# Paired DMA transposes, a tile's blocks side by side, outputs issued by ScalarE, 128 columns last, and a new order in a fused spectral filter and MLP kernel

## The chip, the cores and the metric

The kernel runs on one core of a Trainium2 chip. The metric is the time of one execution on the device in microseconds (us), the median of several runs. A profile of one execution shows the five engines: TensorE (PE, with its weight loads as PEld), VectorE (DVE), ScalarE (ACT), GpSimd (POOL) and SyncE (SP). SP and ScalarE also issue DMAs, shown as SPq and ACTq.

## The reference

`A_x` has 2048 rows of 512 values in bfloat16. Two results of it are mixed, row by row, with a gate:

```
x = A_x
g = sigmoid((x * gate_w).sum(-1, keepdims=True))
X = rfft2(x.astype(float32), axes=(-2, -1)) * (A_w_r + 1j * A_w_i)
a = irfft2(X, s=(2048, 512), axes=(-2, -1)).astype(bfloat16)
h = einsum("bsd,df->bsf", x, B_w1) + B_b1
act = h * tanh(softplus(h))
b = einsum("bsf,fd->bsd", act, B_w2)
out = g * a + (1 - g) * b
```

`B_w1` is 512 x 1792, `B_w2` 1792 x 512, and `A_w_r`, `A_w_i` are 2048 x 257.

## The kernel before

The rows are cut into 16 tiles of 128 (tile t holds the rows t, t+16, t+32 and so on, L447), and four tiles make a chunk c. All of the work is a list of named tasks, each with its engine, its reads and writes and the PSUM banks it needs. A string, `ORDER` (L300), gives one order of all tasks; the tokens of one engine, in their order, are that engine's program. A token is name:engine:bank. Before an instruction an engine waits on semaphores for the tasks that it depends on and for the last users of its bank (`place`, L221, and `emit`, L259). A token's place in the string sets nothing across engines beyond that.

The tasks by name, with number 0 to 15 for a tile where one stands:

- `x0`, `x2`, `x4`, `x8`, `x12` load x (L516), from 2 to 4 tiles each; `w1_*` and `w2_*` load the MLP's weights, `wr..s.` and `wi..s.` (L532) the filter's weights into a staging area, in six pieces of 257 KB, two of 249 and two of 8, `ldM` and `ldG` (L617, L619) constant matrices of 512 KB, `cFD` (L513) one of 128 KB.
- The MLP wants x transposed, in `xT`. Tiles 0 to 7 are transposed on TensorE (`tr`, L552 and L554, four matmuls of 128 columns) and copied out of PSUM (`evx`, L475, on ScalarE or VectorE). Tiles 8 to 15 are transposed by a DMA from HBM (`xt`, L534 and L462). `m{c}_{f}` (L800) is the first layer for chunk c and one of 14 pieces of 128 hidden units: four matmuls of 512 columns. The first four pieces of chunk 0 run as halves a and b. `h{c}_{f}` (L805, ScalarE) applies bias and activation. `n{t}` (L828) is the second layer for a tile, 14 matmuls of 512 columns; for tile 15 it is two tasks, `n15_0` with 384 columns and `n15_384` with 128.
- The spectral half runs in stages with DMAs between them: `bf` (L567, VectorE, sums and differences of x; bf4 and later do four tiles at once) and `p` (L577), `d` (L591), the shuffle DMAs `sh` (L613), `t` (L676), the filter on VectorE (`p1`, `p2`, `ad`), the edge step `e1` to `e3` (L709 to L739), `it` (L750), the DMAs `hx` (L758), `id` (L774) and `ip` (L812). The copies out of PSUM are `ep`, `ed`, `et`, `eit` and `ec`, all by L475.
- `gwb`, one matmul of 512 columns (L537), spreads the gate's weights, and `gt` (L599) makes the gate's sums.
- A tile of the output is written twice in SBUF: `o` scales the first of its two parts (L817, L818), and `s` adds the second (L822). Then `out` is issued, for two tiles at once (L846), for tile 14 alone (L848), and for tile 15 in two parts of 384 and 128 columns (L841).

Three things set the order around the change. TensorE, ScalarE and VectorE run their own lists strictly in order. SP's DMAs are issued in order too, and those with data dependencies (`sh`, `wrn`, `hx`, `out`) hold up what is behind them. PSUM has eight banks, and a token's bank is free when its last user is done.

Of the kernel before, what the change touches and what calls it, by code (L numbers as in the profile page):

```python
# [300 lines left out]
cRF:act ones:pool ident:pool ebase:pool x0:sp x2:sp w1_0a:sp warm:pe:0 fl0:pe:1
tr0:pe:0 gwl:act braw:act w1_0b:sp x4:sp bf0_0:dve bf0_1:dve tab:act w1_4:sp
x8:sp tr1:pe:1 evx1:act evx0:dve p0:pe:2 p1:pe tr2:pe:0 w1_9:sp x12:sp
wr0s1:sp wi0s2:sp wi0s0:sp wr0s2:sp cFD:sp wr0s0:sp ldM0:sp bf2_0:dve bf2_1:dve
tr3:pe:1 p2:pe:4 p3:pe tr_b:pe:6 evx3:dve ev_b:dve evx2:act fl1:pe:7 m0_2a:pe:1
m0_1a:pe:0 m0_1b:pe m0_2b:pe m0_3a:pe:6 m0_0a:pe:7 m0_3b:pe m0_0b:pe ep2:act ep0:dve
h0_2:act h0_1:act h0_3:act gwb:pe:0 bf4_0:dve bf4_1:dve tr4:pe:1 evx4:dve p4:pe:2
tr7:pe:6 p5:pe evx7:dve ep4:dve tr5:pe:4 m0_6:pe:1 tr6:pe:6 h0_0:act evx5:act
evx6:dve m0_8:pe:4 bf8_1:dve bf8_0:dve xt8:sp xt9:sp xt10:sp h0_8:act h0_6:act
gwe:act xt11:sp gt0:dve p6:pe:2 m1_8:pe:6 p7:pe p8:pe:4 p9:pe ep8:dve  # L310
ep6:act h1_8:act m0_7:pe:1 h0_7:act m1_7:pe:0 m1_5:pe:2 h1_5:act p10:pe:4 p11:pe
m1_0:pe:1 ep10:act h1_0:act bf12_1:dve bf12_0:dve gt1:dve p14:pe:2 p12:pe:6 p15:pe
p13:pe m1_4:pe:4 m0_4:pe:1 gt2:dve ep12:dve gt3:dve ep14:act d6:pe:2 d14:pe:6
gt4:dve h1_7:act h1_4:act h0_4:act ldM1:sp d7:pe gt5:dve d2:pe:4 d15:pe
# [7 lines left out]
gt14:dve h0_12:act h1_10:act t0_0:pe:2 gt15:dve wip0:pool wip1:pool wim000:dve zcl:dve
t0_1:pe wi1s0:sp wr1s0:sp et0:act m0_9:pe:1 ez:pool wrm010:dve wr1s1:sp wi1s1:sp
m1_11:pe:0 wrp0:pool wrp1:pool m2_8:pe:4 h1_11:act h2_8:act wim011:dve wim001:dve wim010:dve
t3_0:pe:2 t3_1:pe et3:act h2_4:act h2_6:act m1_6:pe:0 m2_7:pe:4 h2_0:act h2_7:act
h0_9:act h1_6:act xt12:sp xt13:sp ez1:dve win0:dve wic0:dve wiz0:dve xt14:sp
xt15:sp wrn00:sp wrn01:sp t2_0:pe:2 t2_1:pe p20_0:dve:0 et2:dve wim110:dve m2_1:pe:5
# [12 lines left out]
h3_6:act ad_6:dve p1_5:dve p27_0:dve:2 p27_1:dve ad_4:dve p1_7:dve ad_5:dve ad_7:dve  # L340
edge:sp e1:pe:2 o2_0:dve n0_0:pe:6 h3_2:act xp1:dve:0 xp20:dve:1 xp21:dve ead:dve:2
o0_0:act e2:pe:5 e3:dve m3_8:pe:4 ldG1:sp inv:sp ldG2:sp ldG0:sp it2_0:pe:0
it1_0:pe:2 ldG3:sp it1_1:pe it0_0:pe:6 it2_1:pe it0_1:pe eit1:dve eit0:dve h3_8:act
eit2:act n3_0:pe:4 it5_0:pe:0 it5_1:pe it3_0:pe:2 it3_1:pe eit3:dve eit5:act it4_0:pe:6
it4_1:pe n15_384:pe:5 eit4:act it6_0:pe:0 it6_1:pe it7_0:pe:2 it7_1:pe eit6:dve eit7:act
hx4_1:act hx4_0:act o3_0:act n4_0:pe:6 o4_0:dve hx12_0:act n5_0:pe:4 id6:pe:0 hx12_1:sp
rft:sp hx8_1:sp id7:pe o5_0:dve ec6:dve:0 id4:pe:2 id5:pe ec4:act:1 n7_0:pe:6
ey6_1:dve ey6_0:dve ey4_1:dve ey4_0:dve id12:pe:0 id13:pe id14:pe:2 id15:pe ip4:pe:4
n12_0:pe:7 s4:dve hx8_0:sp hx0_0:sp o7_0:act ec14:act:0 ey14_1:dve ec12:act:1 hx0_1:act
ey12_0:dve ey12_1:dve ip13:pe:4 id10:pe:0 id11:pe ip12:pe:6 ec10:act:1 o13:act o12:act  # L350
ey14_0:dve ey10_0:dve ey10_1:dve s12_0:dve ip15:pe:2 o15:dve n11_0:pe:3 id8:pe:0 id9:pe
ip11:pe:2 ip5:pe:4 id0:pe:6 id1:pe s15_384:dve n13_0:pe:5 ec8:act:0 s5:dve ey8_0:dve
ey8_1:dve ec0:act:1 out15_384:sp ey0_0:dve ey0_1:dve id2:pe:0 id3:pe ip10:pe:4 ip14:pe:6
o14:dve out5:sp n14_0:pe:7 o10:act o11:dve s11_0:dve s13_0:dve ip6:pe:6 n10_0:pe:5
ip1:pe:4 ec2:act:0 ey2_0:dve s14_0:dve ey2_1:dve ip3:pe:7 ip2:pe:0 ip9:pe:1 ip8:pe:3
n8_0:pe:2 s10_0:dve s1:dve s6:dve o9:act out11:act s3:dve s2:dve out3:act
ip7:pe:0 ip0:pe:1 o8:dve s0:dve s7:dve out1:act out7:act n9_0:pe:3 s9_0:dve
# [4 lines left out]
def _build(nc, A_x, A_w_r, A_w_i, B_x, B_w1, B_b1, B_w2, gate_w, out, XTP=8, LATE=8, NWARM=13, TRM=4,
# [10 lines left out]
    with es:  # L373
# [163 lines left out]
        G.add("gwb", "small", dict(pe=lambda e: e.matmul(bank(gb), one[0:1, :], junk[0:1, :], start=True, stop=True)), ("pe", 1, 512), reads=["gwl"], writes=[gb])  # L537
# [6 lines left out]
        for t in range(XTP):  # L544
            b = _Buf("b1")

            def f_tr(e, t=t, b=b):
                ins = None
                for dt_ in range(4):
                    xs = x_sb[:, t, 128 * dt_:128 * (dt_ + 1)]  # L550
                    if t < TRM:
                        ins = e.matmul(bank(b)[:, 128 * dt_:128 * (dt_ + 1)], xs, identt[:, :], start=True, stop=True)  # L552
                    else:
                        ins = e.transpose(bankb(b)[:, 128 * dt_:128 * (dt_ + 1)], xs, identt[:, :])  # L554
# [235 lines left out]
        for c in range(NCH):  # L790
            dph = {0: [], 1: [], 2: t_sh, 3: t_mv}[c]
            for ft in range(NFT):
# [3 lines left out]
                for h in ((0, 1) if split else (2,)):  # L796
                    def f_mm1(e, c=c, ft=ft, b=b, h=h):
                        ins = None
                        for dt_ in (range(4) if h == 2 else range(2 * h, 2 * h + 2)):
                            ins = e.matmul(bank(b), w1_sb[:, dt_, 128 * ft:128 * (ft + 1)], xT[:, c, dt_, :, :], start=(dt_ == 0), stop=(dt_ == 3))  # L800
# [98 lines left out]
```

## Time and profile before

| | us |
|---|---|
| median of 3 runs | 131.04 (130.96 to 131.35) |
| the profiled execution | 130.94 |
| its span (first to last event) | 129.17 |
| PE busy | 124.5, 96% of the span |
| DVE busy | 95.6, 74% |
| ACT busy | 71.8, 56% |
| share of TensorE's clock granted | 1.0 |

The span is what the profile's clock shows of that execution; 1.77 us of its time lie around it. "Busy" of PE is made of modelled ends: a matmul of 512 columns is shown with 0.38 us, while the next begins earlier. The chain that ended last is the path followed back from the last instruction.

### The profile page before, as it was taken

The page shows a single profiled execution, that of the slowest core. Times are in us where ns is not written, and L with a number is a line of the kernel's source. Part 1 is how long each engine was busy: PE and PEld are TensorE (multiplying, and loading weights), DVE is VectorE, ACT ScalarE, POOL GpSimd, SP SyncE. Part 2 cuts the span into 40 slices and gives each one's busy share as a digit, 9 for nine tenths or more (in the row PEclk, how much of TensorE's full clock was granted, in tenths as well). Part 3 has the DMA queues.
Part 4 walks back from the last instruction along what each step waited for, and adds up shares of the span by engine and source line. Part 5 has one row for each costly group of instructions (what it writes and reads, how often), then busy time and mean ns, then how long its engine had stood idle before and what let it go on. Part 6 is the DMA issues. An engine that isn't in the chain of part 4 may idle for free.

```text
span 129.2 us, 2150 instructions
## 1 busy us (share of the span) xinstructions
PE 124.5 (96%) x841; PEld 68.1 (53%) x856; DVE 95.6 (74%) x164; ACT 71.8 (56%) x101; POOL 5.8 (5%) x13
## 2 busy tenths in 40 slices
PE   7999999999999999999999999998999999999992
PEld 5645656765555544346544447583556554544450
DVE  0748699999997999999799833463196679677851
ACT  3556689979799999999930275273015331302000
POOL 2000000000077000000000000000000000000000
PEclk9999999999999999999999999999999999999999
DMA  3999999919999999999159200004902002032243
GB/s 89 308 334 396 251 209 138 252 51 327 296 271 155 183 219 338 360 266 228 41 134 274 119 0 0 0 5 154 391 33 77 9 0 91 0 122 81 81 167 112
DMA packets 16759, 21.20 MB, mean 164 GB/s; under 512 B 5805, under 2 KB 11694, under 8 KB 16686
## 3 DMA queue, kind: packets, MB, share of 16 engines
q1 hardware_dynamic: 15280, 18.84, 55.8%
q10 hardware_dynamic: 1470, 2.23, 4.7%
q8 instruction: 7, 0.11, 0.4%
q14 instruction: 2, 0.02, 0.0%
HBM read 12.66 MB, written 2.10 MB: 114 GB/s over the span
## 4 chain that ended last, share of the span: by engine, by line
PE 88%; DMA 3%; ACT 3%; DVE 1%; ACTq 1%; issue 1%; SPq 0%
PE ps L800 36%; PE ps L828 35%; DMA rA<-in_A_x_dram 3%; PE ps L750 3%; PE ps L676 3%; PE ps L591 3%; PE ps L774 3%; PE ps L812 3%; PE ps L577 2%; ACTq L463 1%; ACT hs L805 1%; ACT rF L475 1%; PE ps L554 1%; ACT rC L475 1%; DVE rB L567 1%
## 5 line engine op out<-in xcount | busy, mean ns | idle before, releaser
L800 PE MATMUL ps<-rX,w_sb 128*128 128x512 bf16 x215 | 50.3, 379 | 0.5
L800 PEld LDWEIGHTS ps<-rX,w_sb 128*128 128x128 bf16 x224 | 20.7, 98 | 21.9 <-ACT rD L805 1.1
L828 PE MATMUL ps<-w_sb,hs 128*128 128x512 bf16 x109 | 24.9, 379 | 0.6 <-ACT rX L817 0.4
L805 ACT ACTIVATE hs<-ps,b1f 128x512 bf16<-128x512 f32 x28 | 18.4, 697 | 5.0 <-PE ps L800 4.9
L828 PEld LDWEIGHTS ps<-w_sb,hs 128*128 128x128 bf16 x112 | 10.8, 98 | 13.0 <-ACT rX L817 0.9
L828 PE MATMUL ps<-w_sb,rS 128*128 128x512 bf16 (+2 forms) x70 | 12.9, 336 | 0.0
L828 PE MATMUL ps<-w_sb,rD 128*128 128x512 bf16 x55 | 12.5, 379 | 0.1
L599 DVE SCALAR_TENSOR_TENSOR w_sb<-rA,w_sb 128x512 bf16<-128x512 bf16 x16 | 11.0, 688 | 1.4 <-ACT w_sb L475 1.0
L689 DVE TENSOR_TENSOR tmp<-rC,rA 64x1024 bf16<-64x1024 bf16 x16 | 10.7, 685 | 1.1 <-ACT rC L475 0.6
L475 ACT ACTIVATE rC<-ps 128x1024 bf16<-128x1024 f32 x11 | 11.2, 1034 | 0.3 <-PE ps L577 0.3
L817 ACT ACTIVATE rX<-ps,omg 128x512 bf16<-128x512 f32 x5 | 3.4, 687 | 13.7 <-PE ps L828 12.0
L784 DVE TENSOR_TENSOR rA<-tmp,ps 128x512 bf16<-128x512 f32 x16 | 10.1, 679 | 1.3 <-ACT tmp L475 1.2
L567 DVE TENSOR_TENSOR rB<-rA 128x1024 bf16<-128x1024 bf16 (+1 forms) x10 | 5.4, 580 | 5.7 <-DMA rA<-in_A_x_dram 5.5
L475 ACT ACTIVATE tmp<-ps 128x512 f32<-128x512 f32 x7 | 4.1, 595 | 9.6 <-PE ps L774 9.6
L828 PEld LDWEIGHTS ps<-w_sb,rS 128*128 128x128 bf16 x70 | 6.3, 98 | 5.6
L822 DVE SCALAR_TENSOR_TENSOR rX<-ps,omg,rX 128x512 bf16<-128x512 f32 (+2 forms) x9 | 6.0, 688 | 4.1 <-PE ps L828 4.0
L805 ACT ACTIVATE rD<-ps,b1f 128x512 bf16<-128x512 f32 x14 | 8.9, 717 | 0.3 <-PE ps L800 0.3
L805 ACT ACTIVATE rS<-ps,b1f 128x512 bf16<-128x512 f32 x14 | 8.8, 721 | 0.3 <-PE ps L800 0.3
L828 PEld LDWEIGHTS ps<-w_sb,rD 128*128 128x128 bf16 x56 | 5.5, 98 | 6.6 <-DVE rX L822 0.2
L817 ACT ACTIVATE rX<-ps,gcol 128x512 bf16<-128x512 f32 x4 | 2.6, 686 | 9.2 <-PE ps L812 6.2
L475 DVE CAST rF<-ps 128x1024 bf16<-128x1024 f32 x4 | 4.8, 1222 | 3.8 <-PE ps L750 3.8
L822 DVE SCALAR_TENSOR_TENSOR rX<-ps,gcol,rX 128x512 bf16<-128x512 f32 x8 | 5.6, 745 | 2.3 <-PE ps L812 2.3
(78 smaller groups left out, 132.3 us busy)
## 6 DMA issues: line engine op xcount, KB each, us to landing
w_sb<-in_B_w_dram SPq DMA_DIRECT2D x4, 640.0 KB, 9.6
rF<-c_m SPq DMA_DIRECT2D x4, 512.0 KB, 6.6
rE<-rD SPq DMA_DIRECT2D x8, 256.0 KB, 2.6
rB<-c_g SPq DMA_DIRECT2D x4, 512.0 KB, 6.4
rA<-in_A_x_dram SPq DMA_DIRECT2D x3, 512.0 KB, 9.1
rW<-rW SPq DMA_DIRECT2D x4, 260.0 KB, 7.5
rC<-rF ACTq DMA_DIRECT2D x4, 256.0 KB, 3.3
rC<-rF SPq DMA_DIRECT2D x4, 256.0 KB, 3.7
```

The source lines that it names most:

```text
L475: fns = dict(dve=lambda e: e.tensor_copy(out=o(), in_=i()), act=lambda e: e.activation(o(), i(), AF.Copy))
L567: return e.tensor_tensor(out=xu[:, a:b_, uv, :], in0=x_sb[:, a:b_, 0:256], in1=x_sb[:, a:b_, 256:512], op=ALU.add if uv == 0 else ALU.subt ...
L591: ins = e.matmul(o[:, 2 * e_:2 * e_ + 2, uv, :], zu[:, c, g, :], FD[:, c, :].rearrange("p (r k) -> p r k", r=2), start=True, stop=True)
L599: t_gt.append(dve(f"gt{t}", "gate", "stt", 512, lambda e, t=t: e.scalar_tensor_tensor(out=junk, in0=x_sb[:, t, :], scalar=1.0, in1=gwr, op ...
L676: ins = e.matmul(bank(b, i)[:, 128 * k:128 * (k + 1)], Mm[:, f, :], In[:, _fin(f), :], start=True, stop=True)
L689: return e.tensor_tensor(out=zv(z)[lo], in0=Y[hi, f0:f0 + 8, :], in1=Wi[hi, f0:f0 + 8, 0:128], op=ALU.mult)
L784: return e.tensor_tensor(out=yb[:, t:t + 2, 256 * h:256 * h + 256].rearrange("p t (i e) -> p t i e", e=2), in0=t4(z), in1=o4(bank(b, 1)), ...
L800: ins = e.matmul(bank(b), w1_sb[:, dt_, 128 * ft:128 * (ft + 1)], xT[:, c, dt_, :, :], start=(dt_ == 0), stop=(dt_ == 3))
L805: G.add(f"h{c}_{ft}", "mish", dict(act=lambda e, c=c, ft=ft, b=b: e.activation(hs[c][:, ft, :], bank(b), AF.Mish, bias=b1f[:, ft:ft + 1])) ...
L817: f_a = lambda e: e.activation(o_()[0], o_()[1], AF.Copy, scale=o_()[2])
L822: dve(name, "fin", "psums", hi - lo, lambda e: e.scalar_tensor_tensor(out=bs[:, t, lo:hi], in0=bank(b)[:, 0:hi - lo], scalar=col[:, t:t + ...
L828: ins = e.matmul(bank(b)[:, 0:hi - lo], hs[c][:, ft, 128 * tl:128 * (tl + 1)], w2_sb[:, ft, lo:hi], start=(ft == 0), stop=(ft == NFT - 1))
```

## The change

There are four edits and a new `ORDER`, in which nearly every line differs; the diff shows its end.

1. A transposing DMA takes two neighbouring tiles at once: four DMAs (xt8, xt10, xt12, xt14) of 128 rows by 1024 values instead of eight of 128 by 512.
2. So that such a pair is one stretch in SBUF, `xT` is laid out by chunk, tile, block and column instead of chunk, block, tile and column. `evx` writes 512 columns in a row instead of four runs of 128, and a matmul of the first layer reads its 512 moving columns as four runs of 128.
3. All outputs are issued by ScalarE. Before, five of ten were SP's.
4. `n15_384`, `s15_384` and `out15_384` come last; before, the three were early and `n15_0`, `s15_0` and `out15_0` came last.

```
-s8_0:dve out13:sp out14:sp out9:sp n15_0:pe:0 s15_0:dve out15_0:act
+out1:act out5:act out13:act n9_0:pe:3 s9_0:dve n15_0:pe:5 n15_384:pe:4 out9:act s15_0:dve
+out15_0:act s15_384:dve out15_384:act
...
-        xT = rX[:].rearrange("p (c a t m) -> p c a t m", c=NCH, a=4, t=4)
+        xT = rX[:].rearrange("p (c t a m) -> p c t a m", c=NCH, a=4, t=4)
...
-        for t in range(XTP, NT):
-            dma(f"xt{t}", xT[:, t // 4, :, t % 4, :], xv[:, t, :], queue=("sp",), transpose=True, kb=128, writes=[("xT", t)])
+        for t in range(XTP, NT, 2):
+            dma(f"xt{t}", xT[:, t // 4, t % 4:t % 4 + 2, :, :].rearrange("p t a m -> p (t a) m"), xv[:, t:t + 2, :].rearrange("p t d -> p (t d)"),
+                queue=("sp",), transpose=True, kb=256, writes=[("xT", t), ("xT", t + 1)])
...
-            evac(f"evx{t}", lambda t=t: xT[:, t // 4, :, t % 4, :], lambda b=b, t=t: (bank(b) if t < TRM else bankb(b)[:, 0:512]).rearrange("p (a c) -> p a c", a=4), 512, [b], [("xT", t)], "trm" if t < TRM else "tr")
-        for t in range(XTP, NT):
+            evac(f"evx{t}", lambda t=t: xT[:, t // 4, t % 4, :, :], lambda b=b, t=t: (bank(b) if t < TRM else bankb(b)[:, 0:512]).rearrange("p (a c) -> p a c", a=4), 512, [b], [("xT", t)], "trm" if t < TRM else "tr")
+        for t in range(XTP, NT, 2):
...
-                            ins = e.matmul(bank(b), w1_sb[:, dt_, 128 * ft:128 * (ft + 1)], xT[:, c, dt_, :, :], start=(dt_ == 0), stop=(dt_ == 3))
+                            ins = e.matmul(bank(b), w1_sb[:, dt_, 128 * ft:128 * (ft + 1)], xT[:, c, :, dt_, :], start=(dt_ == 0), stop=(dt_ == 3))
```

One line is new, so that lines behind L533 carry a number that is higher by one in the changed kernel.

The start of TensorE's list, behind the warm-up, before the change (L552 and L554 are `tr`, L577 `p`, L800 the first layer, L537 `gwb`):

```order
L552 MATMUL ps<-identt,rA 128x128 x8
L577 MATMUL ps<-w_sb,rB 128x128 x8
L552 MATMUL ps<-identt,rA 128x128 x8
L577 MATMUL ps<-w_sb,rB 128x128 x8
L540 MATMUL ps<-identt,w_sb 128x14
L498 MATMUL ps<-const-bfloat16-1.0 128x128 x2
L800 MATMUL ps<-rX,w_sb 128x512 x16
L537 MATMUL ps<-w_sb,const-bfloat16-1.0 128x512
L554 MATMUL ps<-identt,rA 128x128 x4
L577 MATMUL ps<-w_sb,rB 128x128 x4
```

The same place of TensorE's list in the changed kernel:

```order
L553 MATMUL ps<-identt,rA 128x128 x8
L578 MATMUL ps<-w_sb,rB 128x128 x8
L553 MATMUL ps<-identt,rA 128x128 x8
L578 MATMUL ps<-w_sb,rB 128x128 x8
L541 MATMUL ps<-identt,w_sb 128x14
L498 MATMUL ps<-const-bfloat16-1.0 128x128 x2
L801 MATMUL ps<-rX,w_sb 128x512 x10
L555 MATMUL ps<-identt,rA 128x128 x12
L801 MATMUL ps<-rX,w_sb 128x512 x2
L555 MATMUL ps<-identt,rA 128x128 x4
L801 MATMUL ps<-rX,w_sb 128x512 x2
L538 MATMUL ps<-w_sb,const-bfloat16-1.0 128x512
```

The transposes of tiles 4, 5 and 7, which need `x4`, stand behind 10 matmuls of the first layer instead of behind 16 and `gwb`, and no `p` stands between them.

SP's list from the loads of x on, as a difference (rS is the staging area of the filter's weights, w_sb from c_front is `cFD`, rF from c_m `ldM`, rX the transposed x, rE from rD `sh`):

```order
-L463 DMA rS<-in_A_w_r_dram 16x8224
-L463 DMA rF<-c_m 128x2048
-L462 DMA_TRANSPOSE rX<-in_A_x_dram 128x4x128 x4
-L463 DMA rF<-c_m 128x2048
-L463 DMA rE<-rD 128x1x1024 x4
+L463 DMA rS<-in_A_w_i_dram 16x32x257
+L463 DMA rS<-in_A_w_i_dram 16x8224
 L463 DMA rS<-in_A_w_i_dram 16x31x257
```

All ten pieces of the filter's weights (eight of them large) now stand ahead of the transposes; before, three large ones stood there, with `ldM0`. The transposes then stand in one row, followed by `ldM0` and the shuffles:

```order
L463 DMA rS<-in_A_w_r_dram 16x8224
L462 DMA_TRANSPOSE rX<-in_A_x_dram 128x8x128 x4
L463 DMA rF<-c_m 128x2048
L463 DMA rE<-rD 128x1x1024 x2
L463 DMA rF<-c_m 128x2048
L463 DMA rE<-rD 128x1x1024 x6
```

So the pairs for chunk 3 are loaded before the shuffles and no longer behind them.

The end of ScalarE's list in the changed kernel, from its outputs on (L818 is `o`, L463 an output):

```order
L463 DMA out_dram<-rX 128x1024 x2
L463 DMA out_dram<-rX 128x512
L463 DMA out_dram<-rX 128x1024
L818 ACTIVATE rX<-ps,gcol 128x512 x2
L463 DMA out_dram<-rX 128x1024 x4
L463 DMA out_dram<-rX 128x384
L463 DMA out_dram<-rX 128x128
```

Before, that list ended with four outputs of 128x1024 and the one of 128x384, and no ScalarE work stood behind an output. The part of 128 columns is now the last.

In the middle, o0_0 and o3_0 went from ScalarE to VectorE; `n5_0` follows `id11` instead of `n4_0`, and between the last `it` and the first `id` stand `n0_0` and `n14_0`. Six of the eight `it` tiles run in a row, in the order 1, 0, 5, 2, 6, 7, behind `m2_7`; then come `m2_13` and the other two. Before, second-layer groups stood between them.

More of the change, by code (lines that the diff above doesn't have):

```diff
@@ L300 @@
 ORDER = """
[L301 to L314, printed above, removed]
@@ L322 @@
[L322 to L327, printed above, removed]
@@ L340 @@
[L340 to L357, printed above, removed]
-s8_0:dve out13:sp out14:sp out9:sp n15_0:pe:0 s15_0:dve out15_0:act
+cRF:act ones:pool wrp1:pool ebase:pool wrp0:pool ident:pool x0:sp bf0_1:dve bf0_0:dve
@@ new lines @@
+x2:sp warm:pe:0 fl0:pe:1 tr0:pe:0 gwl:act braw:act tr1:pe:1 p0:pe:2 w1_0a:sp
+tab:act evx0:act evx1:act w1_0b:sp x4:sp p1:pe tr2:pe:0 bf2_0:dve bf2_1:dve
+tr3:pe:4 p2:pe:6 evx3:act p3:pe ep2:act w1_4:sp x8:sp w1_9:sp tr_b:pe:1
+evx2:dve fl1:pe:5 m0_1a:pe:0 m0_0a:pe:4 m0_0b:pe m0_3a:pe:5 m0_3b:pe ev_b:dve ep0:dve
+tr4:pe:1 bf4_1:dve evx4:dve tr5:pe:2 tr7:pe:3 m0_1b:pe tr6:pe:1 m0_2a:pe:6 evx6:act
+evx7:act h0_0:act evx5:dve gwb:pe:7 bf4_0:dve gwe:dve gt0:dve gt1:dve gt2:dve
+bf8_1:dve x12:sp wr0s2:sp m0_2b:pe m0_5:pe:1 m1_7:pe:4 h0_2:act h0_5:act h0_3:act
@@ new lines @@
+xt14:sp m3_0:pe:7 m3_8:pe:5 m3_10:pe:3 m3_11:pe:0 m3_13:pe:1 h1_9:act wim000:act wrm010:dve
+wim110:dve wim111:dve wim001:dve h3_0:act h3_8:act m3_9:pe:2 h3_9:act wip1:pool wip0:pool
+m3_6:pe:7 ldM0:sp sh0_1:sp h3_13:act h3_11:act m3_1:pe:5 m1_12:pe:2 sh0_3:sp ldM1:sp
+sh0_0:sp sh0_2:sp t1_0:pe:0 t1_1:pe h3_10:act h1_12:act h3_6:act h1_6:act sh1_2:sp
+win1:dve sh1_1:sp wic1:dve h3_1:act win0:dve wic0:dve ez:pool sh1_0:sp sh1_3:sp
+wiz0:dve et1:dve p21_0:dve:0 m3_12:pe:3 h3_12:act m2_4:pe:2 t3_0:pe:0 t3_1:pe wiz1:dve
@@ new lines @@
+m2_2:pe:7 h2_2:act xp21:dve xp1:dve:1 ead:dve:2 e2:pe:4 o6_0:dve e3:dve o3_0:dve
+m2_7:pe:6 h2_7:act it1_0:pe:2 ldG3:sp ldG1:sp ldG2:sp it1_1:pe eit1:act it0_0:pe:4
+it0_1:pe eit0:dve it5_0:pe:0 it5_1:pe eit5:act it2_0:pe:6 it2_1:pe eit2:dve it6_0:pe:2
+it6_1:pe eit6:act it7_0:pe:4 it7_1:pe eit7:act m2_13:pe:0 it3_0:pe:6 it3_1:pe eit3:dve
+it4_0:pe:2 it4_1:pe n0_0:pe:1 n14_0:pe:6 eit4:act hx8_0:act hx8_1:act h2_13:act hx12_0:act
+hx4_0:act hx4_1:sp hx12_1:act id8:pe:2 id9:pe id10:pe:4 id11:pe o0_0:dve n5_0:pe:7
@@ L359 @@
+o12:act id4:pe:0 id5:pe ip7:pe:6 ip6:pe:3 ec4:act:0 ey4_0:dve ip2:pe:2 s2:dve
+out3:act ey4_1:dve n11_0:pe:5 s6:dve s11_0:dve ip15:pe:7 out11:act s7:dve out14:act
+out7:act ip0:pe:3 ip13:pe:2 o15:act ip5:pe:0 ip1:pe:1 n8_0:pe:5 ip4:pe:4 n12_0:pe:7
+n13_0:pe:6 s12_0:dve s5:dve s1:dve s0:dve o13:act s13_0:dve s4:dve s8_0:dve
+out1:act out5:act out13:act n9_0:pe:3 s9_0:dve n15_0:pe:5 n15_384:pe:4 out9:act s15_0:dve
+out15_0:act s15_384:dve out15_384:act
 """
```

51 lines of the change are left out of this document (32 added, 19 removed).

## Prediction

> **What bounds the kernel now.** I read the page's busy times first, then the chain of work that ended last, then the groups of instructions, then the timeline at the places the change touches.
>
> ```profile
> span 129.2 us, 2150 instructions
> PE 124.5 (96%) x841; PEld 68.1 (53%) x856; DVE 95.6 (74%) x164; ACT 71.8 (56%) x101; POOL 5.8 (5%) x13
> PE 88%; DMA 3%; ACT 3%; DVE 1%; ACTq 1%; issue 1%; SPq 0%
> 43.32 7.34 PE ps L800 x34
> 79.28 1.34 PE ps L750 x24
> ```
>
> TensorE carries 88% of the last chain. The two chain rows give its pace: 7.34/34 = 0.216 us for a matmul of 512 columns, 1.34/24 = 0.056 us for one of 128. Counted in the program from the first MLP matmul on, there are 451 matmuls of 512 columns, 14 of 384 (2.27 us by the tail rows below) and 334 of 128: 97.4 + 2.3 + 18.7 = 118.4 us. The first starts at 6.86 and the last ends at 126.80, so of 119.9 us some 1.5 are not matmul pace. The change has the same matmuls in the same numbers. It can only move three things: waits of TensorE (at most 1.5 us to win, any amount to lose), the time before 6.86, and what follows TensorE's end.
>
> **The start.**
>
> ```profile
> 3.87 0.76 DVE L567 TENSOR_TENSOR rB<-rA 128x512 bf16<-128x512 bf16 x2 [3.87 <-DMA rA<-in_A_x_dram]
> 5.26 0.76 DVE L567 TENSOR_TENSOR rB<-rA 128x512 bf16<-128x512 bf16 x2
> 6.02 0.69 DVE L475 CAST rX<-ps 128x512 bf16<-128x512 f32 x1
> 6.81 3.18 PEld L800 LDWEIGHTS ps<-rX,w_sb 128*128 128x128 bf16 x16
> 7.08 3.40 PE L800 MATMUL ps<-rX,w_sb 128*128 128x512 bf16 x15
> 9.78 1.29 DVE L567 TENSOR_TENSOR rB<-rA 128x1024 bf16<-128x1024 bf16 x2 [1.63 <-DMA rA<-in_A_x_dram]
> 10.41 0.09 PEld L537 LDWEIGHTS ps<-w_sb,const-bfloat16-1.0 1*128 1x128 bf16 x1 [0.42 <-issue]
> 10.73 0.23 PEld L554 LDWEIGHTS ps<-identt,rA 128*128 128x128 bf16 x4 [0.23 <-issue]
> 11.12 0.23 PEld L577 LDWEIGHTS ps<-w_sb,rB 128*128 128x128 bf16 x4 [0.17 <-DVE rB L567]
> 11.17 0.42 DVE L475 COPY rX<-ps 128x512 bf16<-128x512 bf16 x1
> ```
>
> Up to the first MLP matmul both programs run the same TensorE list. What it waits for last is two `bf` of VectorE from 5.26, when `x2` has landed, and one copy of a transposed tile until 6.71; in the change that copy is evx2 instead of evx3, of the same size. One record of the 16 is missing (15 in the row from 7.08), so the matmuls begin one pace earlier, at 6.86. I cost the start at nothing. SP's first nine issues are unchanged, so `x4` lands when it did: VectorE waits for it until 9.78.
>
> Before, 16 MLP matmuls and `gwb` ran while `x4` was on its way. The change puts `tr4` behind ten: 6.86 + 10 x 0.216 = 9.02, and TensorE then waits for `x4` until 9.80: **+0.78**. Before, gaps at the same place were smaller: 7.08 + 15 x 0.216 = 10.32 to 10.41; 10.63 to 10.73; 10.95 to 11.12: 0.36 together, and these go, since `p4` now comes after 28 MLP matmuls and no longer meets its `bf4`. Next in line there is `tr6`, whose bank waits for evx4, which VectorE does behind bf4_1: 9.80 + 0.64 (half of 1.29) + 0.42 = 10.86, while TensorE arrives at 9.80 + 12 x 0.056 + 2 x 0.216 = 10.90. Net at the start: **+0.42**.
>
> **The middle.**
>
> ```profile
> 86.69 1.02 ACT L475 ACTIVATE rF<-ps 128x1024 bf16<-128x1024 f32 x1 [0.63 <-PE ps L750]
> 86.70 2.97 PE L828 MATMUL ps<-w_sb,hs 128*128 128x512 bf16 x13
> 87.80 1.52 ACTq L463 DMA_DIRECT2D rC<-rF  x2
> 89.37 0.69 ACT L817 ACTIVATE rX<-ps,omg 128x512 bf16<-128x512 f32 x1 [1.66 <-issue]
> 90.11 3.20 PE L828 MATMUL ps<-w_sb,hs 128*128 128x512 bf16 x14 [0.44 <-ACT rX L817]
> rC<-rF ACTq DMA_DIRECT2D x1, 256.0 KB, 3.3
> ```
>
> Before, `n5_0` needs the bank that o3_0 empties, and o3_0 stands on ScalarE behind the issues of two `hx` DMAs. n4_0 starts one pace before 86.70 (a record is missing) and would be done at 86.48 + 14 x 0.216 = 89.50; n5_0 starts at 90.11. These 0.61 go, since the change gives o3_0 and o0_0 to VectorE: **-0.61**.
>
> What is late next is `id8`, which needs hx8_0 and hx8_1. TensorE covers them with n0_0 and n14_0, 28 x 0.216 = 6.05 us. From the last `it` matmul on, its tail (0.16), the evacuation (1.02) and its handing over take 1.3 us, and ScalarE's second `hx` lands 0.65 + 3.3 us after the first is issued: 5.25 us, 0.8 to spare, which one more `hx` of SP's ahead of it could use up. I cost it at nothing. In the `it` stage the change runs six tiles in a row on four pairs of banks: it6 comes 4 x 0.45 = 1.79 us after it1 began, but eit1, behind h2_7 on ScalarE, is done at 0.16 + 0.69 + 1.02 = 1.87 (the 0.69 is the row at 89.37, a tile of the same size), and it7 meets eit0 in the same way: **+0.15**, an estimate from these rows.
>
> **The tail.**
>
> ```profile
> 105.39 0.35 DVE L822 SCALAR_TENSOR_TENSOR rX<-ps,omg,rX 128x128 bf16<-128x128 f32 x1
> 121.49 5.31 PE ps L828 x28
> 126.82 0.62 DVE L822 SCALAR_TENSOR_TENSOR rX<-ps,omg,rX 128x384 bf16<-128x384 f32 x1 [0.86 <-PE ps L828]
> 127.47 0.34 ACTq L463 DMA_DIRECT2D out_dram<-rX  x1
> out_dram<-rX SPq DMA_DIRECT2D x1, 32.0 KB, 1.5
> out_dram<-rX ACTq DMA_DIRECT2D x1, 96.0 KB, 1.7
> ```
>
> After TensorE's end at 126.80 come the 384-column sum (0.62), ScalarE's issue and 1.7 us to landing: 129.17. Of the chain's 5.31 us for 28 matmuls, 14 of 512 are 3.02, which leaves the 2.3 for those of 384 columns. With 128 columns last (0.78 us of TensorE), s15_0 runs under them and ends 0.14 before TensorE does; out15_0 is issued 0.10 before and occupies ScalarE's queue until 0.24 after. s15_384 takes 0.02 + 0.35, its issue comes at 0.41, and 32 KB land in 1.5: 1.9 us after TensorE's end, not 2.37. **-0.47**. It is lost in part if an issue that follows another on ScalarE is long: the two `hx` issues took 1.52 together, 0.76 each, and then the last one starts 0.25 later. That SP's outputs move to ScalarE costs nothing else: behind out3, out11, out14 and out7 stand only o15 and o13, and the next to ask for their banks is n12_0, more than 14 matmuls (3.0 us) after `ip15`.
>
> **Transposes and loads.**
>
> ```profile
> 4.82 1.46 SPq L463 DMA_DIRECT2D rA<-in_A_x_dram  x1
> rA<-in_A_x_dram SPq DMA_DIRECT2D x1, 512.0 KB, 13.1
> 19.46 3.23 SPq L462 DMA_TRANSPOSE rX<-in_A_x_dram  x1
> rX<-in_A_x_dram SPq DMA_TRANSPOSE x1, 10.2
> rX<-in_A_x_dram SPq DMA_TRANSPOSE x1, 5.3
> 34.20 0.62 SPq L463 DMA_DIRECT2D rE<-rD  x1
> rE<-rD SPq DMA_DIRECT2D x1, 256.0 KB, 2.9
> 36.82 0.63 SPq L463 DMA_DIRECT2D rS<-in_A_w_i_dram  x1
> rS<-in_A_w_i_dram SPq DMA_DIRECT2D x1, 257.0 KB, 6.4
> ```
>
> The first transpose (issued at 13.10) landed after 10.2 us, at 23.3, and the fourth at 19.46 + 5.3 = 24.8: 0.5 us a tile. The trace has no pair; between 0.5 (one tile's price) and 2.0 (twice the price a tile) I take 1.0, the row's price for two. Issuing is held up by the data ahead (3.23 us for one), so SP's own time isn't what counts.
>
> In the change five more pieces of the weights (about 257 KB each) stand ahead of xt8 and xt10, and ldM0 no longer does. Four such pieces landed between 34.20 + 2.9 = 37.1 and 36.82 + 6.4 = 43.2: 1.53 us each. So xt10 lands by 24.8 + 5 x 1.53 = 32.4. TensorE reaches m2_11, which needs it, after 93 matmuls of 512 and 124 of 128: 6.86 + 20.1 + 6.9 + 0.78 = 34.6. **Spare 2.2 us: no cost.** t1_0 comes at 6.86 + 149 x 0.216 + 128 x 0.056 + 0.78 = 47.0 and needs sh0, which SP issues once xt14 (34.4) is nearly through: about 40 with ldM0 and 2.9 to land, 7 to spare.
>
> **The matmul's operand in pieces.** The 224 matmuls of L800 now read four runs of 128 columns instead of 512 in a row.
>
> ```profile
> 74.88 0.27 PE L710 MATMUL ps<-rC,rD 128*128 128x63 bf16 x1
> 74.97 0.18 PE L709 MATMUL ps<-rC,rD 128*128 128x1 bf16 x1
> 78.19 0.22 PE L735 MATMUL ps<-tmp,rD 128*128 128x63 bf16 x2
> ```
>
> L710 reads each of 63 columns 256 bytes from the last and takes 0.09 us to the next start; L735 reads 63 in a row, which at the pace of 512 is 63/512 x 0.216 = 0.03, and its two in 0.22 us agree with that. That is 0.06 us for 62 jumps, about 1 ns each. With three jumps in each of 224 matmuls the upper end is 0.65 us, the lower 0 (nothing there could be faster). I take 0: a run here is 256 bytes long and the slow row's 2, so the contiguous row is the nearer one.
> The Trainium skill ("SBUF — State Buffer", section "Door 1: The DMA port swizzle") has lines of 16 bytes, at full bandwidth while accesses stay in a line and a penalty when they cross: by it L710's columns pay one each, which the rows agree with, and whole lines in runs pay no more than contiguous ones, so the term is 0; counted per jump it would be 0.65.
>
> **Sum.** The profiled execution took 130.94, its span 129.17 (1.77 around it); the median of the runs is 131.04, 0.10 above. 130.94 + 0.42 - 0.61 + 0.15 - 0.47 = 130.43. Of the 1.5 us above, 0.5 are neither the start nor n5_0 but the edge matmuls and small hand-overs; the new order has spares as small as 0.03, and I allow 0.1 more of these, an estimate: **130.5**.
>
> **Rivals.** *The gain is eaten*: ScalarE's last issue is late (+0.25), and small waits come to 0.3 instead of 0.1: 131.0. For it speaks that the landing of `x4` now decides a wait of TensorE directly. *Pieces cost*: +0.65, 131.1, as now; from about 0.7 ns a jump the gain is gone. *The transposes come late* (slower): the weights' pieces or the pairs are slower than their rows, and m2_11 waits. It decides from (34.6 - 24.8)/5 = 1.96 us a piece, or from 1.56 with pairs at 2.0. At 2.3 us a piece xt10 lands at 36.3 and TensorE waits 1.7: 132.2. Against it speaks that `x12` landed at 4.82 + 13.1 = 17.9 and the first transposed tile at 23.3, so that three pieces, the constant cFD, ldM0 and that tile took 5.4 together; for it, that pieces of both kinds and transposes now meet in one queue all at once. *`x4` comes early*: without its wait the start gives -0.36 instead of +0.42, 129.7; nothing ahead of it in SP's queue changes, so little speaks for that. And the change may not do what it says: a pair carried out as two single transposes, with two issues' time on SP. That gives 130.5 too, since nothing waits for them.
>
> **How the numbers follow.** Forecast 0.49, `x4` early 0.05, gain eaten 0.17, pieces cost 0.06, late transposes 0.23. About 0.3% (0.39 us) is what a measurement of this kernel can tell from no change; 0.07 of the forecast's chance lies inside it. Faster 0.42 + 0.05 = 0.47, same 0.07 + 0.17 + 0.06 = 0.30, slower 0.23. The range goes from 129.9, above the early `x4`, to the late transposes at 132.2; half of that rival's chance may lie beyond. The forecast's own range is 130.1 to 130.8.
>
> **What would show it.** In the changed profile: VectorE's first 1024-column `bf` and TensorE's L555 start together near 9.8 with TensorE idle from 9.0; no idle time before a L829 near 90; TensorE's end within 0.3 us of 126.8, the last sum 128 columns wide and the last landing 1.9 us behind it; L801 at 0.216 us a matmul. I am wrong if TensorE stands near 34.6 waiting for a DMA into rX, if L801's pace is above 0.217, or if the last issue is long.

## The result, and the profile after

The changed kernel takes 130.61 us (median of 22 runs, 129.28 to 132.69) where the kernel before takes 130.91 (22 runs, 130.50 to 131.35). The ratio is 0.9933, 95% interval 0.9912 to 0.9955; this ratio and those below compare only runs within 1.5% of their kernel's fastest, which here leaves out eight of the changed kernel's 22 and none of the 22 of the kernel before, while medians and ranges are of all runs. The medians alone give 0.998, and nine of the changed kernel's 22 runs are longer than the median of before. So the gain is small, and over all runs it is not clear of their spread, which is now 3.4 us instead of 0.85; that spread, which I had not foreseen, is what most of the experiments are about. The forecast was 130.5. The profiled execution took 130.14, its span 128.7.

The page of the changed kernel: the span, the busy times and the chain's shares by engine.

```profile
span 128.7 us, 2154 instructions
PE 124.8 (97%) x849; PEld 68.1 (53%) x856; DVE 94.5 (73%) x164; ACT 70.2 (55%) x101; POOL 4.9 (4%) x13
PE 82%; DMA 11%; SPq 3%; DVE 1%; issue 1%; ACT 1%
```

A DMA now has 11% of the chain that ended last; before it had 3%. The chain itself (start, duration, what; all in us) says which DMA, and how it ends:

```profile
5.10 13.52 DMA rA<-in_A_x_dram
18.61 0.02 issue
18.64 1.30 DVE rB L568 x2
19.94 0.04 issue
19.98 0.40 PE ps L578 x4
...
34.12 3.45 PE ps L801 x16
...
117.53 9.28 PE ps L829 x56
126.80 0.02 issue
126.83 0.35 DVE rX L823
```

The load issued at 5.10 is `x12`. It lands at 18.6, VectorE's two `bf12` follow at once, and `p14` on TensorE, which needs both, follows them. From there to the end of TensorE at 126.80 the chain hardly leaves TensorE. So x12's landing set the end of this execution, and nothing before it did. The first layer's pace is 3.45/16 = 0.216 us, as before, and the last sum is 128 columns wide.

The timeline at the places that the prediction named (start, duration, engine, line, operation; in brackets the idle time before and what ended it):

```profile
9.42 0.69 DVE L568 TENSOR_TENSOR rB<-rA 128x1024 bf16<-128x1024 bf16 x1 [1.32 <-DMA rA<-in_A_x_dram]
9.44 0.84 PE L555 MATMUL ps<-identt,rA 128*128 128x128 bf16 x12 [0.30 <-DMA rA<-in_A_x_dram]
...
10.78 0.59 PE L801 MATMUL ps<-rX,w_sb 128*128 128x512 bf16 x2
11.30 0.39 PE L538 MATMUL ps<-w_sb,const-bfloat16-1.0 1*128 1x512 bf16 x1
11.62 0.61 PE L801 MATMUL ps<-rX,w_sb 128*128 128x512 bf16 x2
...
19.45 0.39 PE L578 MATMUL ps<-w_sb,rB 128*128 128x128 bf16 x4
19.98 0.40 PE L578 MATMUL ps<-w_sb,rB 128*128 128x128 bf16 x4 [0.15 <-DVE rB L568]
...
78.71 3.00 PE L751 MATMUL ps<-rB,rC 128*128 128x128 bf16 x48
...
86.33 3.19 PE L829 MATMUL ps<-w_sb,rS 128*128 128x512 bf16 x14
89.35 1.06 PE L775 MATMUL ps<-rE,rC 128*128 128x128 bf16 x16
90.24 2.97 PE L829 MATMUL ps<-w_sb,hs 128*128 128x512 bf16 x12
```

`bf4` and `tr4` start together, but at 9.43, since x4 landed earlier than in the profile of before. The ten matmuls end their pace at 6.82 + 10 x 0.216 = 8.98 (6.82 is where L801 starts), so the wait is 0.46, not 0.78. (The brackets of these rows count from modelled ends and show less.) The rows at 19.45 and 19.98 are `p11` and `p14`: `p11` is through at 19.45 + 4 x 0.056 = 19.67, and TensorE waits 0.3 us there, which the prediction does not have. Around `gwb` (L538) two small gaps stay: 10.78 + 2 x 0.216 = 11.21 to 11.30, and 11.30 + 0.216 = 11.52 to 11.62. Behind 89.35, `id8` to `id11` and then `n5_0` start without idle time: 89.35 + 16 x 0.056 = 90.25. The wait for o3_0 is gone.

The end: the last two outputs of ScalarE, with the time from issue to landing of the last, then three of the paired transposes.

```profile
126.70 0.85 ACTq L463 DMA_DIRECT2D out_dram<-rX  x2
out_dram<-rX ACTq DMA_DIRECT2D x1, 32.0 KB, 1.5
25.68 4.10 SPq L462 DMA_TRANSPOSE rX<-in_A_x_dram  x1
rX<-in_A_x_dram SPq DMA_TRANSPOSE x1, 7.6
29.83 1.31 SPq L462 DMA_TRANSPOSE rX<-in_A_x_dram  x1
rX<-in_A_x_dram SPq DMA_TRANSPOSE x1, 5.4
31.18 2.06 SPq L462 DMA_TRANSPOSE rX<-in_A_x_dram  x1
rX<-in_A_x_dram SPq DMA_TRANSPOSE x1, 5.1
```

TensorE ends at 126.80 in both kernels; the last landing comes 1.9 us later instead of 2.37. ScalarE's last two issues took 0.85 us together, so the rival of a late last issue did not come. xt10 lands at 25.68 + 7.6 = 33.3, and m2_11, which needs it, starts four matmuls behind the 34.12 of the chain, at 35.0: no wait there, with 1.7 to spare. xt12 and xt14 land at 35.2 and 36.3, 1.1 us apart; xt8 had landed at 30.8, 2.4 us before xt10.

### The profile page after: what moved, and what is told of

Read it like the earlier page. It is cut to its first block, busy times and chain, and to the rows that moved or that the text cites. A ratio compares the mean times of both kernels' runs of the same rounds, so it can differ in the third digit from the quotient of the medians.

```text
span 128.7 us, 2154 instructions
## 1 busy us (share of the span) xinstructions
PE 124.8 (97%) x849; PEld 68.1 (53%) x856; DVE 94.5 (73%) x164; ACT 70.2 (55%) x101; POOL 4.9 (4%) x13
## 3 DMA queue, kind: packets, MB, share of 16 engines
q10 hardware_dynamic: 2334, 3.45, 7.4%
## 4 chain that ended last, share of the span: by engine, by line
PE 82%; DMA 11%; SPq 3%; DVE 1%; issue 1%; ACT 1%
PE ps L829 37%; PE ps L801 30%; DMA rA<-in_A_x_dram 11%; SPq L463 3%; PE ps L751 3%; PE ps L677 3%; PE ps L592 3%; PE ps L813 2%; PE ps L775 2%; DVE rB L568 1%; PE ps L578 1%; ACT rX L818 1%; DVE rX L823 0%; PE ps L711 0%; PE ps L736 0%
## 5 line engine op out<-in xcount | busy, mean ns | idle before, releaser
L801 PE MATMUL ps<-rX,w_sb 128*128 128x512 bf16 x224 | 52.7, 379 | 0.0
L801 PEld LDWEIGHTS ps<-rX,w_sb 128*128 128x128 bf16 x224 | 20.7, 98 | 20.3 <-issue 0.4
L475 DVE CAST rC<-ps 128x1024 bf16<-128x1024 f32 x5 | 6.1, 1222 | 2.3 <-PE ps L578 1.4
L818 ACT ACTIVATE rX<-ps,gcol 128x512 bf16<-128x512 f32 x5 | 3.2, 684 | 7.7 <-DVE rX L823 5.3
L475 ACT ACTIVATE rD<-ps 128x1024 bf16<-128x1024 f32 x7 | 7.0, 1030 | 0.0
L475 ACT ACTIVATE tmp<-ps 128x512 f32<-128x512 f32 x5 | 2.9, 596 | 6.7 <-PE ps L775 6.7
L818 ACT ACTIVATE rX<-ps,omg 128x512 bf16<-128x512 f32 x4 | 2.7, 684 | 6.9 <-PE ps L829 6.9
```

Of the source, the lines that this page charges most:

```text
L475: fns = dict(dve=lambda e: e.tensor_copy(out=o(), in_=i()), act=lambda e: e.activation(o(), i(), AF.Copy))
L818: f_a = lambda e: e.activation(o_()[0], o_()[1], AF.Copy, scale=o_()[2])
```

## The experiments

The question is where the 3.4 us of spread come from, and whether the terms of the prediction are the right ones. **Theory A**: x12's landing sets TensorE's progress and varies from run to run. **Theory B**: the pairs land late in some runs and hold TensorE up near 35. **Theory C**: it is x4's landing. All ratios are to the kernel before, measured beside each on the same chip, where its median was 131.0 to 131.2 us. Where a cut shows no `:engine`, it gives the order of the tokens by their names alone.

### x12 may land later (A against B)

```
-p11 ep10 bf12_0 bf12_1 gt3 p14 m1_3 p15 m1_10 p9 ep14 h1_10 gt4 gt5 ep8 gt6 p12 p13 m1_13 m0_6 gt7 ep12
+p11 ep10 p9 bf12_0 bf12_1 ep8 m1_3 m1_10 p14 p15 h1_3 h1_10 ep14 gt3 p12 p13 ep12 m0_6 h0_6 m1_13 gt4 gt5 gt6 gt7
```

> The changed kernel with the first spectral stage of tiles 14 and 15 put behind eight first-layer matmuls and tile 9's, so that x12 may land 1 us later. Theory A (the landing of x12 sets TensorE's progress, and the changed kernel's runs spread because it varies): the gap of 0.37 us between two L578 near 19.6 goes, the median falls by 0.3 to 0.6 us, and the runs of 129.3 to 132.7 us draw together to about 1 us. Theory B (the paired transposes land late in some runs and hold TensorE up near 34.9): the gap goes, but the median falls by at most 0.3 us and the spread of about 3.4 us stays. Theory C (the landing of x4 sets it): nothing changes, since the gap near 9.4 stays.

Measured: 0.9914 (0.9883 to 0.9945), median 130.09 (129.46 to 131.57), nine of ten runs within 1.2 us. x12 landed late as ever (18.4 us) and cost nothing; the pairs were not touched (xt10 at 32.3), and nothing waited for them. That speaks for A and against B: with x12's users moved back, most of the spread is gone. C is not touched by it.

### The pairs ahead of the weights

```
-cFD:sp ... wr1s0:sp ... xt8:sp xt10:sp xt12:sp
+cFD:sp xt8:sp xt10:sp ... wr1s0:sp ... xt12:sp
```

> The changed kernel with the two paired transposes of chunk 2 issued right behind cFD, ahead of seven pieces of the filter's weights. They should land near 22 us instead of 33.3, 12 us before their first use. Theory A: the gap at 19.6 stays or grows, spread and median stay within 0.2 us. Theory B: the spread falls to about 1 us and the median falls by 0.4 us or more. A cost of its own could come from the weights landing 1 to 2 us later, which VectorE's filter preparation would show as a wait for a DMA near 28 us.

Measured: 0.9903 (0.9865 to 0.9941), median 130.05, six runs from 129.60 to 130.20. By the expectation's words that is B's outcome. But the edit took more away than I had thought: with the transposes behind it, x12 landed at 15.7 us, 3 us earlier than in the changed kernel. So this run doesn't tell A from B, and it points at something else: what stands behind x12 in SP's list bears on when x12 lands. One profile can't tell that from chance (a short run of the unaltered list, below, has 15.7 too), but x12 landed at 15.4 and 16.0 in the two other versions with the pairs there, shown last.

### The changed kernel again

> The changed kernel once more, unaltered, for the runs beside it: a median 0.2 to 0.5 us under the kernel before, runs from 129.3 to 132.7 us. Theory A: in whatever execution the profile catches, the span is about 1.3 us plus the landing of x12 longer than in the shortest one: x12 at 18.6 goes with a span of 128.7, x12 at 19.9 with about 130.

Measured: 0.9978 (0.9943 to 1.0012), median 130.89 (131.04 beside it), runs from 129.91 to 132.25. The spread is there again; the gain, 0.15 us of the median, is under what was expected and can't be told from none. x12 landed at 18.6 and the span was 128.6, as A has it, though the chain of this execution starts with x4 (below).

### The weights' pieces in two other orders

```
-cFD wi1s1 wi1s0 wi0s1 wr0s0 wr1s1 wr0s1 wi0s0 wi0s2 wr1s0
+cFD wi1s0 wr0s0 wi0s0 wr1s0 wi1s1 wi0s1 wr1s1 wr0s1 wi0s2
```

> The changed kernel with another order of the filter's weights behind cFD: the four pieces of 16 rows with 16 KB each first, then the four that are moved in packets of 514 bytes. If it is these small packets that hold up the slowest engine's share of x12 (theory A1), x12 lands near 16.5 us, the gap at 19.6 goes, the median falls by 0.4 us or more and the spread shrinks. If any data behind x12 do it (A2), x12 lands at 18.4 to 20 as in the changed kernel, and time and spread stay.

Measured: 0.992 (0.9893 to 0.9948), median 129.91 against 130.89 for the unaltered change beside it, nine runs within 1.4 us. x12 landed at 17.0.

```
-cFD wi1s1 wi1s0 wi0s1 wr0s0 wr1s1 wr0s1 wi0s0 wi0s2 wr1s0
+cFD wi1s1 wi0s1 wr1s1 wr0s1 wi1s0 wr0s0 wi0s0 wr1s0 wi0s2
```

> The opposite order of the same pieces: the four in packets of 514 bytes first, then the four of 16 KB. A1: x12 lands at 20 us or later, TensorE's gap near 20 grows past 1 us and the median rises to 131.5 or more. A2: x12 lands at 18.4 to 20, and the time stays within 0.3 us of the changed kernel's.

Measured: 0.9962 (0.9936 to 0.9988), median 130.64 (129.69 to 131.42), x12 at 17.3. A1 expected 20 us and 131.5, and A2 an x12 of 18.4 or more: both missed, though A2's time (within 0.3 us of the changed kernel's 130.89) held. The order matters, as the version with the 16-KB pieces first shows, but "small packets first makes it worse" doesn't hold for the time.

What the loads did is seen in the traffic. The next three rows are the stretch from 15 to 18 us in three kernels. Their columns are the stretch, its length, the busy time of PE, PEld, DVE, ACT and POOL with their instructions, the granted clock, the busy share of the DMA engines and the GB/s that they moved. First the kernel before:

```profile
15.00:18.00 3.00, 3.00 (x25) 1.75 (x23) 1.90 (x4) 3.00 (x5) 0.00 (x0) 1.00 1.02 189
```

The changed kernel:

```profile
15.00:18.00 3.00, 3.00 (x25) 1.70 (x23) 2.05 (x3) 3.00 (x5) 0.00 (x0) 1.00 1.05 120
```

The changed kernel with the 16-KB pieces first:

```profile
15.00:18.00 3.00, 3.00 (x24) 1.65 (x22) 2.21 (x4) 3.00 (x6) 0.00 (x0) 1.00 0.92 236
```

The busy shares are alike, the bytes are not. The trace has 16 completions for each of these loads, and a load counts as landed with the last of them. The load in front of x12 is `w1_9`, so the time from its landing to that of x12 (each its issue plus the time to landing) tells how long the slowest part of x12 took:

| behind x12 | w1_9 landed | x12 landed | between |
|---|---|---|---|
| transposes (pairs first) | 14.4 | 15.7 | 1.3 |
| order of before | 15.3 | 17.9 | 2.6 |
| the same (layout alone) | 13.9 | 17.0 | 3.1 |
| the same (o3_0 on VectorE) | 15.9 | 18.3 | 2.4 |
| 16-KB pieces first | 14.1 | 17.0 | 2.9 |
| 514-byte packets first | 13.8 | 17.3 | 3.5 |
| order of the change | 14.8 | 18.6 | 3.9 |
| the same (changed kernel again) | 15.0 | 18.6 | 3.6 |
| the same (x12 may land later) | 14.6 | 18.4 | 3.9 |
| the same, in a long run (tail undone) | 16.0 | 19.9 | 4.0 |
| the same, in a long run (SP's outputs) | 16.1 | 20.0 | 3.8 |
| the same, in a short run (single tiles) | 13.4 | 15.7 | 2.3 |

Two things add up: the queue is already early or late at w1_9 (13.4 to 16.1), in both kernels, and the order of the change mostly lets x12's slowest part take 3.6 to 4.0 us where that of before took 2.4 to 3.1. What in the mixed order does it stays open.

The single completions show where the time goes. In every profile more than half of x12's 16 are there by 14.6 us; what varies is the last few. In the changed kernel's profile 14 are there by 15.6, and the last two come at 17.8 and 18.6. In the long run with the tail undone 15 are there by 16.0 and the last comes at 19.9. There the last one is behind the one before it by 1.3 us at x4 already, by 2.7 at w1_9 and by 3.9 at x12, so the lag grows down the queue. One DMA engine falling behind would look like that, but it is not shown: the trace doesn't say which engine a completion is from.

### Long runs caught in a profile: the tail undone, and outputs by SP

Two kernels were profiled in one of their long executions, which shows what is long there.

```
-n15_0:pe:5 n15_384:pe:4 out9:act s15_0:dve out15_0:act s15_384:dve out15_384:act
+n15_384:pe:4 n15_0:pe:5 out9:act s15_384:dve out15_384:act s15_0:dve out15_0:act
```

> The changed kernel with its last two pieces swapped: the 384 columns of tile 15 end it again and the 128 columns come before them. By the prediction's tail term it loses 0.47 us against the changed kernel: the last landing is 2.4 us behind TensorE's end instead of 1.87, the last VectorE sum takes 0.62 instead of 0.35, and TensorE's end stays near 126.8. If the last landing were set by ScalarE's issues and not by the width of the last piece, the loss would be under 0.15 us.

```
-out5:act out9:act out13:act out14:act out15_0:act
+out5:sp out9:sp out13:sp out14:sp out15_0:sp
```

> The changed kernel with five outputs (out5, out9, out13, out14 and the 384 columns of tile 15) issued by SP again. By the prediction it makes no difference: the last landing stays 1.9 us behind TensorE's end, and the time within 0.2 us. Rival: ScalarE's last issue was delayed by the one before it, and this saves 0.25 us behind TensorE's end.

Measured: tail undone 0.9957 (0.9918 to 0.9995), median 131.27 (131.23 beside it); outputs by SP 0.9931 (0.9903 to 0.996), median 130.65 (130.99 beside it). The profiled executions took 132.00 and 131.55. The chain of the second, at x12 and at its end:

```profile
5.15 14.80 DMA rA<-in_A_x_dram
...
128.15 0.03 issue
128.17 0.35 DVE rX L823
```

What its TensorE waited for (us in total, times, longest):

```profile
PE ps L578 <- DVE rB L568: 1.2, 2, 1.0
...
PE ps L555 <- DMA rA<-in_A_x_dram: 0.8, 1, 0.8
```

The chain of the kernel with the tail undone:

```profile
5.73 14.22 DMA rA<-in_A_x_dram
...
128.14 0.03 issue
128.16 0.62 DVE rX L823
```

And its waits:

```profile
PE ps L578 <- DVE rB L568: 1.3, 2, 1.1
PE ps L555 <- DMA rA<-in_A_x_dram: 0.6, 1, 0.6
```

In both, x12 lands at 19.95 instead of 18.6, and TensorE ends at 128.14 instead of 126.80: 1.34 us later for a load that landed 1.34 us later. TensorE waits for nothing near 35. So theory A is shown for these two: a long run is a late x12. The very longest runs (up to 133.3) were in no profile.

With TensorE's end alike in both, the tail can be compared too. With the wide piece last the last landing is at 130.48, 2.34 us behind TensorE; with 128 columns last it is at 130.01, 1.86 behind: 0.48. In the medians this can't be told from the spread. And with five outputs issued by SP the end was 1.86 behind TensorE, with all by ScalarE 1.87, so where those five are issued is worth nothing.

### Which load sets the time

In every profile of the changed kernel and of the versions so far, the chain that ended last starts with one load of x; in the changed kernel's it is x12, issued at 5.10. In that of the changed kernel measured again it is x4:

```profile
2.71 6.85 DMA rA<-in_A_x_dram
```

With the 16-KB pieces first it is x2:

```profile
1.26 4.33 DMA rA<-in_A_x_dram
```

And with single tiles (the next section) x2 again, 0.4 us earlier:

```profile
1.26 3.92 DMA rA<-in_A_x_dram
```

| kernel | load | landed | span | difference |
|---|---|---|---|---|
| changed | x12 | 18.6 | 128.7 | 110.1 |
| outputs by SP | x12 | 19.95 | 130.05 | 110.1 |
| changed, again | x4 | 9.55 | 128.65 | 119.1 |
| x12 may land later | x4 | 9.26 | 128.4 | 119.15 |
| pairs first | x2 | 5.96 | 128.7 | 122.7 |
| 16-KB pieces first | x2 | 5.59 | 128.3 | 122.7 |
| single tiles | x2 | 5.18 | 127.9 | 122.7 |
| 514-byte packets first | x2 | 5.31 | 128.26 | 122.95 |

For the order of the change, then, the span is the largest of three sums: x2's landing + 122.7, x4's + 119.1, x12's + 110.1 (where x12's users stand later, the third is smaller). The last row is 0.25 above them: there TensorE also waited 0.3 us for a copy of ScalarE at 63.4. In the two long runs x4 landed at 9.8 and 9.9, which by its sum gives 128.9 and 129.0, 1.0 us and more below their spans: theory C does not make them, though x4 does set shorter executions. The waits don't add. In the changed kernel's profile TensorE waited 0.46 for x4 and then 0.3 for x12; by these sums it would have waited 0.76 for x12 without the first wait, and ended at the same time.

### The layout alone, single tiles, and n5_0

The kernel before with the new layout of `xT` and single transposes:

```
-xT = rX[:].rearrange("p (c a t m) -> p c a t m", c=NCH, a=4, t=4)
+xT = rX[:].rearrange("p (c t a m) -> p c t a m", c=NCH, a=4, t=4)
...
-xT[:, c, dt_, :, :]
+xT[:, c, :, dt_, :]
```

> The kernel before with one edit: the transposed x is laid out by tile, block and column, so that each first-layer matmul reads its 512 columns as four runs of 128; the transposes stay single and the order stays. The prediction's value is 0: 130.9 us, and the first-layer pace stays at 0.216 us a matmul. By its upper end (1 ns a jump) it costs 0.65 us: 131.55, with a pace of 0.219.

Measured: 0.9981 (0.9954 to 1.0007), median 130.94 (131.23 beside it). A stretch of its chain gives the pace, 2.59/12 = 0.216:

```profile
16.53 2.59 PE ps L800 x12
```

The value 0 holds; a cost of 0.65 us (0.5%) is outside the interval.

The changed kernel with eight single transposes in place of the pairs:

```
-xt8:sp xt10:sp xt12:sp ... xt14:sp
+xt8:sp xt9:sp xt10:sp xt11:sp xt12:sp xt13:sp ... xt14:sp xt15:sp
```

> The changed kernel with eight transposes of one tile in place of the four pairs, in the same places and with the same layout. By the prediction nothing waits for the transposes, and the time stays (within 0.2 us); xt11, the last of chunk 2, lands by 33.5 us, as xt10's pair did. If pairs are cheaper or dearer than two singles by more than 1 us each, TensorE shows it as a wait near 34.9.

Measured: 0.9954 (0.9923 to 0.9985), median 131.28 (130.99 beside it), runs from 129.26 to 133.22. Its profile, of the shortest run, has no wait near 35, with xt11 landed at 31.2 us. Its runs spread as those of the change do, with x12's queue unaltered. A difference between singles and pairs can't be told from that spread; that it is no wait near 35 can.

The kernel before with one token changed:

```
-hx4_1:act hx4_0:act o3_0:act n4_0:pe:6
+hx4_1:act hx4_0:act o3_0:dve n4_0:pe:6
```

> The kernel before with one edit: o3_0 goes from ScalarE to VectorE, which is free there. By the prediction's term, n5_0 no longer waits near 90 us and the time falls by 0.61 us, to 130.3, ratio 0.995. Rival: the wait is only passed on (to id6, n7_0 or the sums of VectorE), and the time falls by under 0.2 us.

Measured: 0.9962 (0.9943 to 0.9981), which is 0.50 us (0.25 to 0.75), median 130.57. n4_0 and n5_0 now run in one piece:

```profile
86.91 5.99 PE L828 MATMUL ps<-w_sb,hs 128*128 128x512 bf16 x27
```

### Both reorderings, and the start

> The changed kernel with both reorderings of SP's list: the two pairs of chunk 2 behind cFD, then the weights' pieces with 16 KB a row, then those in packets of 514 bytes. By theory A x12 lands at 15.6 to 17 us, nothing waits for it, and what is left is the wait for x4 at the start (0.46 us): 129.9 to 130.1 us, all runs within 1 us. If the order of the pieces were worth something by itself, it would fall below either of the two edits alone (0.990 and 0.992 of the kernel before).

> The kernel of the run before this one, with the start of TensorE's list changed too: 12 instead of 10 first-layer matmuls ahead of tr4, all four transposes in a row on banks of their own. With nothing waiting for x12, theory A expects the wait for x4 to count again, so that this gains what it takes off it: 0.3 us, 129.6. If something later still sets TensorE's progress, it gains under 0.1.

```
-cFD wi1s1 wi1s0 wi0s1 wr0s0 wr1s1 wr0s1 wi0s0 wi0s2 wr1s0 xt8 xt10 xt12
+cFD xt8 xt10 wi1s0 wr0s0 wi0s0 wr1s0 wi1s1 wi0s1 wr1s1 wr0s1 wi0s2 xt12
...
-tr4:pe:1 bf4_1:dve evx4:dve tr5:pe:2 tr7:pe:3 m0_1b:pe tr6:pe:1 m0_2a:pe:6
+m0_1b:pe tr4:pe:1 evx4:dve tr5:pe:2 tr7:pe:3 tr6:pe:7 evx5:dve evx7:act evx6:act bf4_1:dve m0_2a:pe:6 m0_2b:pe
```

The first two lines are both kernels', the last two the second's alone. Measured: 1.0041 (1.0018 to 1.0065), median 131.67, runs from 130.40 to 132.25, and 0.9978 (0.9953 to 1.0002), median 130.76. Both expectations missed. Each of the two reorderings alone was 0.8 to 1.0% faster than the kernel before; together they are 0.4% slower. In the first kernel x12 landed at 15.4 and nothing waited for it, but its chain now starts with a piece of the weights:

```profile
20.90 8.18 DMA rS<-in_A_w_r_dram
29.08 2.13 issue
31.22 0.71 DVE rW L642
```

And its timeline at the place where TensorE meets that:

```profile
44.80 1.85 ACT L806 ACTIVATE rS<-ps,b1f 128x512 bf16<-128x512 f32 x3 [1.78 <-DVE rA L641]
45.54 1.25 PE L801 MATMUL ps<-rX,w_sb 128*128 128x512 bf16 x5 [1.22 <-ACT rS L806]
```

`wr0s1` is now the last of the large pieces, and VectorE's first step on the filter's weights (L642) waits 2.13 us for it, from 29.08 to 31.22 (its last completion is at 31.13). The staging area rS is free the later for that: `h3_0`, which writes rS, starts at 44.80 and not at 43.49 as in the changed kernel, and TensorE waits for it at 45.5. In the changed kernel the same L642 began at 29.50. So a fourth sum had stood close behind the first three: in both of these profiles the span is wr0s1's landing (31.13 and 31.63) + 98.6, and in the changed kernel's, where wr0s1 landed at 28.8, it comes to 127.4. The gain from the start could not be seen behind it; why the second of these kernels is 0.6% faster than the first, with the same wait in its profile (1.6 us, in the first 1.2), stays open (its profile is of its longest run).

## Why the prediction was right, and what it lacked

- **The bound and the sum.** That TensorE's work decides and only waits, the start and the tail can move held: TensorE ends at 126.80 as in the kernel before, 0.1 from the sum of the terms ahead of the tail (+0.42 - 0.61 + 0.15 + 0.1 = +0.06). That it comes so close is in part luck: the wait for x4 was 0.32 shorter than forecast, and a wait for x12 that the prediction doesn't have put 0.3 back. The median is near the forecast (130.61 and, measured again, 130.89, for 130.5), but of runs that spread over 3.4 us.
- **Start, +0.42.** The direction was right, and the terms were mis-sized. The wait for x4 measured 0.46 (0.78 forecast), for x4 landed at 9.39, and the forecast had TensorE go on at 9.80. In other profiles it landed between 8.5 and 9.95, and the forecast had taken one profile's landing as fixed. Of the old gaps of 0.36 two of 0.1 around `gwb` stayed.
- **The step that failed** is the one on transposes and loads. It counted the weights' pieces against xt10 only ("xt10 lands by 32.4", measured 33.3; "spare 2.2", measured 1.7) and not against x12, the load directly ahead of them. Its users `bf12` and `p14` had 0.4 us to spare with x12 at 17.9, as in the profile before (p14 is reached at 19.67 and waits for x12's landing + 1.36); at 18.6 that was gone, and at 19.95 TensorE lost over 1 us. Its rival of late transposes had the right culprits, weight pieces and loads meeting in one queue, and the wrong victim. In the middle of the runs this costs little, since the wait for x12 swallows that for x4; in the two long ones profiled it costs 1.3 us more. So the median came out right, and the width of the runs did not.
- **n5_0, -0.61**: shown alone as -0.50 (0.25 to 0.75), with no wait put in its place.
- **`it`, +0.15**: 48 matmuls of 128 columns take 48 x 0.056 + 0.16 = 2.85 at their pace, and the row at 78.71 shows 3.00.
- **Tail, -0.47**: measured 0.48 with TensorE's end alike, and 1.9 us from TensorE's end to the last landing as forecast.
- **Operand in four runs, 0**: 0.216 us in both layouts. The Trainium skill ("SBUF — State Buffer", section "Door 1: The DMA port swizzle") has lines of 16 bytes and a penalty for each access that crosses to a new line; runs of 256 bytes are whole lines, so by it they cost what contiguous ones do, and the measurement agrees.
- **Pairs, 1.0 us each**: measured 1.1 between xt12 and xt14 and 2.4 between xt8 and xt10, and no use of pairing is seen in the time. **Outputs by ScalarE, 0**: the end is 1.87 us behind TensorE's with all outputs by ScalarE and 1.86 with five by SP.
- The rival "x4 early" is not a case of its own: x4's landing varies from run to run, and 8.5 us, with no wait, is one of its values.
